# Regrouping q and k of the late chunks on the chip, by ScalarE copies of 32 partitions, in place of a regrouped copy in DRAM

## The chip, the cores and the metric

The kernel runs on 1 core of one Trainium2 chip. The metric is the device time of one execution in microseconds (us). An execution under the profiler gives a span, from the first to the last instruction, and a trace of every instruction and transfer.

## The reference

Two blocks follow each other. The first is a linear attention with a decay per head, over 4 batches, 8 heads, 768 positions and 64 columns a head:

```python
for b in range(nb):                       # blocks of 64 positions
    intra = einsum('bhic,bhjc->bhij', qb, kb) * Dmask
    intra = einsum('bhij,bhjd->bhid', intra, vb)
    inter = einsum('bhid,bhde->bhie', qb * lam_pow, kv_state)
    out[:, :, sl] = intra + inter
    kv_state = lam_block * kv_state + einsum('bhsd,bhse->bhde', kb * rev_pow, vb)
```

Its output, laid out as 3072 tokens of 512 columns, is the `x` of the second block, a sum over 4 experts weighted by normalised probabilities:

```python
for e in range(E):                        # w1[e]: 512 x 1024, w2[e]: 1024 x 512
    out += p[:, e:e + 1] * (maximum(x @ w1[e], 0.0) @ w2[e])
```

Everything is float32.

## The kernel before

The 3072 tokens are worked in three groups of 1024. A pair of a group and an expert is a unit, 12 in all. The products are done by a scheme of seven block products in place of eight, nested once more inside (names `M1` to `M7`, sums `S` and `T`), so that besides TensorE the other engines have many additions. While the products of one unit run, operands of the next ones are made and loaded.

The main loop (from L1850) goes over `at` (unit), `i` (one of seven products) and `x` (eight parts). One pass of the inner loop is called a slot here, and slot number `(at * 7 + i) * 8 + x` is what work around it is hung on. In the first units a slot of even `x` holds a part of `second_product` (L1233, eight matmul passes into a `q` bank), and a slot of odd `x` two inner products of `first_product` (L1174, into the banks `g1` and `g3`, tiles `pg`). What is read out of `g1` and `g3` is shared between VectorE (L117) and ScalarE: a copy at L1187, a seed of a bank from SBUF at L1151, the last part at L1155 or, with a ReLU, L1157; ReLUs in place are L1191 and L1094. Each engine runs its instructions in the order in which the program names them: an instruction that waits holds up all behind it on that engine.

The attention is cut into 24 chunks `n` of 128 positions of one batch (all 8 heads). Chunks 0 to 7 run ahead of the main loop, chunks 8 to 23 inside it, at the slots that `AT` (L888) lists. For a chunk, q and k must stand with the 64 columns of a head on partitions. Chunks up to 11 are turned by TensorE (L727) and copied out of PSUM by ScalarE (L735, L736). Chunks 12 to 23 ("come across", L506) use VectorE's transpose of 32 x 32 blocks (L707) instead. It transposes each block in place, so the blocks must first be moved: partition group `j` has to hold 32 columns of one half of the heads, and along the free dimension the four heads, and the four groups of 32 positions.

Before, this move is done in DRAM. `bring_across` (L490) lists 128 transfers from q and k to a DRAM tile `across`, in pieces of 32 floats; `trickle` (L501) issues them one by one, during the last direct products ahead of the loop and in the loop (L1963), from SyncE's queue or from ScalarE's. `load_across` (L509) then loads two regrouped tiles, `qx` and `kx`, a chunk. Besides, k is loaded as it stands (`kn`, L174), since the states need k with positions on partitions.

The steps of a late chunk with the slot `s` in `AT` are laid out in `attention` (L892). `turns_at` is `s - 7`, at which VectorE's transposes are queued (they go onto the list `lately` and are taken out at later slots) and at which `decayed` (L682) multiplies `kn` in place on GpSimd. Loads of q and k are at `turns_at - 5`, that of v at about `s - 7`, and at `s` stand the chunk's scores (L761, L768) and the values of the chunk before it (L824, L842, read out by L863). For chunks 12 to 23 `turns_at` is 51, 84, 92, 101, 108, 140, 147, 160, 165, 196, 203 and 216.

`small` (L92) takes tiles of 128 x 512 floats from one pool of 42 buffers. The tiles of q and k come from it, and so do the hidden blocks `m` of the products. A tile whose buffer is still in use waits for its last user.

`send` (L109) issues a transfer and adds an estimate of its time to counters by which `pump` (L208) decides when the next piece of background work ("chores": preparing weights on GpSimd, with their loads) is begun.

Of the kernel before, what the change touches and what calls it, by code (L numbers as in the profile page):

```python
# [14 lines left out]
FP32 = mybir.dt.float32  # L15
# [6 lines left out]
def kernel(  # L22
# [30 lines left out]
    nc = tc.nc  # L53

    B, H, S, D = q.shape
    E, DM, F = moe_w1.shape
    NTOK, DOUT = out.shape
    P = nc.NUM_PARTITIONS
    C = P
    BL = C // 2  # L60
    NHP = H // 2
    NCH = S // C
    CPG = 8
    G = CPG * C
    NG = NTOK // G
# [14 lines left out]
    dram = ctx.enter_context(tc.tile_pool(name="sums", bufs=1, space=DRAM))  # L80
# [11 lines left out]
    def small(name):  # L92
        return pool.tile([P, W], FP32, name=name, tag="t")
# [15 lines left out]
    def send(out, in_, by=None):  # L109
        n = 4 * min(packet(out), packet(in_))  # L110
        moved[0] = max(moved[0], now[0]) + 4 * math.prod(out.shape) / n * (9 + n / 25) / 16 / 1714
        if by is None:
            asked[0] = max(asked[0], now[0]) + 0.27
        (by or nc.sync).dma_start(out=out, in_=in_)
# [35 lines left out]
    def where(n):  # L150
        g, x = divmod(n, CPG)
        return (x // 4, x % 4) if g == 0 else (2 * g + x // 2 % 2, 2 * (x // 4) + x % 2)
# [5 lines left out]
    nat = {}  # L158
# [324 lines left out]


    FIRST_ACROSS = CPG + 4
    across = dram.tile([2, P, NHP, B, 16, 32], FP32, name="across")
    pieces = []
    rank = {0: 0, 2: 1, 3: 2, 1: 3}

    def bring_across(b):  # L490
        c = min(where(n)[0] for n in range(FIRST_ACROSS, NG * CPG) if where(n)[1] == b)
        for x, of in enumerate((q, k)):
            for y in range(4):
                for ac in range(NHP):
                    src = of[b, 4 * (y // 2) + ac, c * C:, (y % 2) * 32:(y % 2 + 1) * 32]
                    to = across[x, y * 32:(y + 1) * 32, ac, b, (c - 2) * 4:]
                    pieces.append((rank[b], lambda by, to=to, src=src: send(
                        out=to, in_=src.rearrange("(t p) d -> p t d", p=32), by=by,
                    )))

    def trickle(m=1, by=None):  # L501
        for _ in range(m):
            if pieces:
                pieces.pop(0)[1](by)

    def comes_across(n):  # L506
        return n >= FIRST_ACROSS

    def load_across(n):  # L509
        c, b = where(n)  # L510
        for x, name in enumerate("qk"):
            t = small(f"{name}x")
            send(
                out=t[:].rearrange("p (h c) -> p h c", c=C),
                in_=across[x, :, :, b, (c - 2) * 4:(c - 1) * 4].rearrange("p h t d -> p h (t d)"),
            )
            nat[n, name + "x"] = t

    def load_more(n):
        if not comes_across(n):  # L520
            load(n, "qk")
        else:
            trickle(sum(x <= rank[where(n)[1]] for x, _ in pieces))
            load_across(n)
            load(n, "k")

    first = small("zeros")
    zeros = first[:, 0:P]
# [36 lines left out]
    for r in range(2):  # L565
        for ac in range(NHP):
            h = 4 * r + ac
            nc.vector.tensor_tensor_scan(
                out=s_decay[:, r, ac], data0=lam_bc[:, h:h + 1].to_broadcast([P, BL]), data1=blk_ident,
# [10 lines left out]
    for ac in range(NHP):  # L580
        nc.vector.tensor_tensor_scan(
            out=q_decay[:, ac], data0=lam_q[:, ac:ac + 1].to_broadcast([P, BL]), data1=zeros[:, 0:BL],
# [303 lines left out]

    FILL = {1: 18, 2: 43}
    AT = (34, 40, 47, 53, 58, 91, 99, 108, 115, 147, 154, 167, 172, 203, 210, 223)  # L888
    V_AHEAD = {CPG + 10: 8, CPG + 13: 10}
    steps = []  # L890

    def attention():  # L892

        first, last = CPG, NG * CPG - 1
        for n in range(first, last + 1):
            s = AT[n - first]
            turns_at = s - (7 if comes_across(n) else 4)

            def both(n=n):
                if n > first:  # L900
                    values(n - 1, ("s0", "s1"))
                scores(n, ("q02", "q12"))

            steps.append((turns_at - (5 if comes_across(n) else 7), lambda n=n: load_more(n)))
            steps.append((s - V_AHEAD.get(n, 7), lambda n=n: load(n, "v")))
            steps.append((turns_at, lambda n=n: turn(n, ("s0", "s1"))))
            if comes_across(n):
                steps.append((turns_at, lambda n=n: (decayed(n), nat.pop((n, "k")))))
            steps.append((s, both))
        steps.append((AT[last - first] + 5, lambda: values(last, ("s0", "s1"))))  # L910
        steps.append((AT[last - first] - 14, turn_gates))
        steps.sort(key=lambda s: s[0])
# [888 lines left out]
        lambda: own_weights("M1"), sum_own("S1", "A21", "A22", ALU.add), *w2_steps[0:4], mine["M1"], *w2_steps[4:],  # L1801
        raw["A12"],
    ))
    for b in rank:
        bring_across(b)
    for m in SEQ0[2:]:
        if m == SEQ0[-1]:
            for _ in range(2):
                feed2(*fill2.pop(0))
        work = direct_product(m, blocks, ("g1", "g3")) if m != "M5" else [m5[1], *m5[3:]]  # L1810
        for x, f in enumerate(work):
            f()
            for y in sums_then.get((m, x), ()):
                y()
            rest()
            if x < len(work) - 1:
                now[0] += 1
                take(own_sums)
                pump(0.75)
            trickle()  # L1820

    start, w1_steps = now[0], prepare_w1(2)

# [26 lines left out]
    for at, (g, e) in enumerate(units):  # L1850
# [14 lines left out]
        for i in range(7):  # L1865
# [18 lines left out]
            else:  # L1884
                b = second_product(g, e, SEQ2[i], banks)
# [21 lines left out]
            for x, part in enumerate(order):  # L1907
                for f in part:
                    if f:
                        f()  # L1910
                now[0] += 1
                put = False
                if at == 0:
                    idle[:] = [("s0", "s1"), i < 3]
                    put = put_back()
                    take(own_sums)
                if nested and ahead:
                    idle[1] = x in ((1, 4) if i < 5 or at > NEST + 1 else (4,)) and (at - 2 * E + 1, i, x) not in held_at
                    put = put_back()
                added = first_steps.pop((at - 2 * E + 1, i, x), None)  # L1920
                if added:
                    added()
                all_added(now[0])
                if joins and not background:
                    joined()
                elif added and x > 2 or put:
                    pass
                elif (ahead or x % 2 == 0 and x + i) and not (nests and i == 6 and x == 7):
                    if nested or nests:
                        if lately:  # L1930
                            take(lately)
                        else:
                            rest()
                        if at == 2 * E and i in (2, 3) and fits():
                            rest()
                    else:
                        took = False
                        for of in (lately, background, own_sums):
                            if of and (not took or fits() or of is background and len(of) > 4):
                                take(of)  # L1940
                                if of is lately and i == 0:
                                    take(of)
                                took = True
                if nested or nests:
                    take(aside)
                    if own_sums and (nested or fits()):
                        take(own_sums)
                if ending and fits():
                    end_first()
                if nested and ahead and x in (1, 3) and fill3:  # L1950
                    feed3(*fill3.pop(0))
                if turned_back and x > 0:
                    for y in turned_back.pop(0):
                        if SEQ3[i] == END[1]:
                            give(*y[:2], ("s0", "s1"), *y[2:])
                        else:
                            give_across(*y)
                if fill and at * 7 + i >= 6 and x in ((0, 1) if at * 7 + i < 13 else (1, 3, 5) if at * 7 + i == 13 else FEED[nested]):
                    feed(*fill.pop(0))
                while steps and (at * 7 + i) * 8 + x == steps[0][0]:  # L1960
                    steps.pop(0)[1]()
                if at == 0 or x % 2 or at == 1 and x == 4:
                    trickle(1, nc.scalar if x % 2 else None)  # L1963
                for h in range(1, NG):
                    if x == 3 and 0 <= at * 7 + i - FILL[h] < 7:
                        x_fill(h, SEQ[at * 7 + i - FILL[h]])
                pump(PACE[g])
# [30 lines left out]
```

## Time and profile before

| what | value |
|---|---|
| median of 3 runs | 1142.18 us (1140.82 to 1142.65) |
| the profiled execution's own time | 1142.07 us |
| its span | 1140.3 us |
| mean granted TensorE clock | 0.999 |
| busy: TensorE, its weight loads, VectorE, ScalarE, GpSimd | 1130.5, 988.2, 769.0, 380.3, 761.0 us |
| transfers of `across`: issued by SyncE, by ScalarE | 61, 67 |
| size of one: 64 of 64 KB, 64 of 32 KB | 6.3 MB in all |
| loads of `qx` and `kx` | 24 of 256 KB, median 4.8 us to landing |
| loads of `kn` as it stands, late chunks | 12 of 256 KB, median 5.1 us to landing |
| VectorE's transposes of `qx` and `kx` | 24, median 700 ns each |

Busy time of an engine is the time in which at least one of its instructions runs; overlapping instructions count once. A wait in the profile is the time an engine stood idle before an instruction, put down to whatever released it last. A transfer's time to landing runs from its issue to its last byte. The share "DMA" is that of the 16 transfer engines' time in which they work at packets.

### The profile page before, as it was taken

The page shows a single profiled execution, that of the slowest core. Times are in us where ns is not written, and L with a number is a line of the kernel's source. Part 1 is how long each engine was busy: PE and PEld are TensorE (multiplying, and loading weights), DVE is VectorE, ACT ScalarE, POOL GpSimd, SP SyncE. Part 2 cuts the span into 40 slices and gives each one's busy share as a digit, 9 for nine tenths or more (in the row PEclk, how much of TensorE's full clock was granted, in tenths as well). Part 3 has the DMA queues.
Part 4 walks back from the last instruction along what each step waited for, and adds up shares of the span by engine and source line. Part 5 has one row for each costly group of instructions (what it writes and reads, how often), then busy time and mean ns, then how long its engine had stood idle before and what let it go on. Part 6 is the DMA issues. An engine that isn't in the chain of part 4 may idle for free.

```text
span 1140.3 us, 22080 instructions
## 1 busy us (share of the span) xinstructions
PE 1130.5 (99%) x7983; PEld 988.2 (87%) x7983; DVE 769.0 (67%) x1474; ACT 380.3 (33%) x768; POOL 761.0 (67%) x730
## 2 busy tenths in 40 slices
PE   8999999999999999999999999999999999999998
PEld 7888888888888888888888888888888888888887
DVE  4576776587577658737655566878767576776785
ACT  3325123212312321232343442444354452342332
POOL 2838147644843786447687997994996873873885
PEclk9999999999999999999999999999999999999999
DMA  9795889999899989769557858886577757657552
GB/s 204 180 287 166 212 222 279 291 270 335 262 292 320 316 291 282 222 222 314 177 177 261 283 180 281 290 272 204 180 264 244 218 162 207 194 160 211 171 194 74
DMA packets 326828, 267.12 MB, mean 234 GB/s; under 512 B 153216, under 2 KB 270144, under 8 KB 326720
## 3 DMA queue, kind: packets, MB, share of 16 engines
q1 hardware_dynamic: 289472, 258.14, 73.1%
q10 hardware_dynamic: 37216, 7.57, 3.5%
q8 instruction: 64, 1.05, 0.4%
q14 instruction: 44, 0.36, 0.1%
q0 software_dynamic: 32, 0.00, 0.0%
HBM read 197.97 MB, written 73.96 MB: 238 GB/s over the span
## 4 chain that ended last, share of the span: by engine, by line
PE 98%; DVE 1%; issue 0%; DMA 0%; ACT 0%; DVEq 0%; POOLq 0%; ACTq 0%
PE pg L1174 41%; PE pq L1550 25%; PE q L1233 21%; PE pM L1692 2%; PE pc L1692 2%; PE op L824 1%; PE sp L761 1%; PE op L842 1%; PE sp L768 1%; PE pM L1417 1%; PE pg L1550 1%; PE qp L727 1%; PE kp L727 0%; DMA decay<-in_lam_dram 0%; PE yp L1377 0%
## 5 line engine op out<-in xcount | busy, mean ns | idle before, releaser
L1174 PE MATMUL pg<-xs,ws_in 128*128 128x256 f32 x1960 | 470.1, 380 | 0.0
L1174 PEld LDWEIGHTS pg<-xs,ws_in 128*128 128x128 f32 x1960 | 371.1, 190 | 52.8 <-DVE m L117 2.4
L117 DVE TENSOR_TENSOR m<-pg,m 128x512 f32<-128x512 f32 x374 | 255.4, 685 | 92.4 <-PE pg L1174 82.5
L1233 PE MATMUL q<-w2t,m 128*128 128x256 f32 x1120 | 265.6, 380 | 0.0
L1233 PEld LDWEIGHTS q<-w2t,m 128*128 128x128 f32 x1120 | 211.7, 190 | 29.3 <-issue 0.3
L117 DVE TENSOR_TENSOR sums<-pq,sums 128x256 f32<-128x256 f32 x272 | 112.9, 420 | 90.6 <-PE pq L1550 76.9
L1550 PE MATMUL pq<-acc,w2t 128*128 128x256 f32 x688 | 169.2, 379 | 0.0
L117 POOL TENSOR_TENSOR m<-m,decay 128x512 f32<-128x512 f32 x91 | 114.5, 1270 | 78.7 <-ACT m L1191 52.1
L1550 PEld LDWEIGHTS pq<-acc,w2t 128*128 128x128 f32 x688 | 130.6, 190 | 17.9
L1191 ACT ACTIVATE m<-m 128x512 f32<-128x512 f32 x99 | 62.4, 630 | 192.5 <-DVE m L117 190.6
L1251 DVE SCALAR_TENSOR_TENSOR acc<-q,gate,acc 128x256 f32<-128x256 f32 x108 | 52.0, 482 | 79.1 <-PE q L1233 78.6
L117 DVE TENSOR_TENSOR m<-m,m 128x512 f32<-128x512 f32 x108 | 92.9, 861 | 6.5 <-ACT m L1157 6.5
L1187 ACT COPY m<-pg 128x512 f32<-128x512 f32 x88 | 51.5, 585 | 122.0 <-PE pg L1174 108.7
L1151 ACT COPY pg<-m 128x512 f32<-128x512 f32 x77 | 45.4, 590 | 113.0 <-DVE m L117 103.3
L117 POOL TENSOR_TENSOR acc<-hT,hT 128x512 f32<-128x512 f32 x56 | 70.3, 1272 | 15.0 <-PE pq L1550 9.9
L117 POOL TENSOR_TENSOR acc<-hT,acc 128x512 f32<-128x512 f32 x56 | 71.2, 1272 | 6.4 <-PE pq L1550 2.7
L1550 PE MATMUL pq<-hT,w2t 128*128 128x256 f32 x288 | 70.0, 379 | 0.0
L117 POOL TENSOR_TENSOR w2o<-w2b 128x512 f32<-128x512 f32 x26 | 33.9, 1325 | 45.8 <-DMA w2b<-in_moe_w_dram 39.3
L1550 PEld LDWEIGHTS pq<-hT,w2t 128*128 128x128 f32 x288 | 54.7, 190 | 7.4
L1155 ACT COPY m<-pg 128x512 f32<-128x512 f32 x44 | 25.7, 585 | 89.6 <-PE pg L1174 84.8
L1550 PE MATMUL pq<-m,w2t 128*128 128x256 f32 x228 | 55.4, 379 | 0.0
L1005 ACT COPY hp<-m 128x512 f32<-128x512 f32 x84 | 48.5, 589 | 15.6 <-DVE hT L117 14.1
(157 smaller groups left out, 1419.5 us busy)
## 6 DMA issues: line engine op xcount, KB each, us to landing
ws_in<-w_ops SPq DMA_DIRECT2D x40, 512.0 KB, 5.1
w2t<-w_ops SPq DMA_DIRECT2D x72, 256.0 KB, 3.2
ws_in<-w_ops SPq DMA_DIRECT2D x60, 256.0 KB, 3.5
ws_in<-w_ops SPq DMA_DIRECT2D x40, 384.0 KB, 4.0
w2b<-in_moe_w_dram SPq DMA_DIRECT2D x56, 256.0 KB, 5.0
w_ops<-ops SPq DMA_DIRECT2D x28, 512.0 KB, 5.5
w_ops<-ops SPq DMA_DIRECT2D x54, 256.0 KB, 4.3
w2t<-w_ops SPq DMA_DIRECT2D x100, 128.0 KB, 2.8
```

What stands on the lines that cost most here:

```text
L117: eng.tensor_tensor(out=o, in0=a, in1=b, op=op)
L727: nc.tensor.transpose(out=x[:, ac * C:(ac + 1) * C], in_=y[:, ac].rearrange("p r d -> p (r d)"), identity=ident[:],)
L1005: nc.scalar.copy(out=there[x][:], in_=blk[at][:])
L1151: nc.scalar.copy(out=banks[tags[1]][:], in_=new["11"][:])
L1155: nc.scalar.copy(out=o[:], in_=p[:])
L1174: nc.tensor.matmul(out=p[:, j * 256:(j + 1) * 256], lhsT=ws[i][:, j * P:(j + 1) * P], rhs=xs[i], start=(fresh and j == 0), stop=True, skip ...
L1187: nc.scalar.copy(out=new[at][:], in_=p[:])
L1191: nc.scalar.activation(out=new[at][:], in_=new[at][:], func=AF.Relu)
L1233: nc.tensor.matmul(out=p[:, s * DH:(s + 1) * DH], lhsT=h[A_OF[m]][:, c * 256 + s * P:c * 256 + (s + 1) * P], rhs=fed2[g, e, m][uu][:, c], ...
L1251: nc.vector.scalar_tensor_tensor(out=o, in0=x, scalar=w, in1=o, op0=ALU.mult, op1=ALU.add)
L1550: nc.tensor.matmul(out=p[:, 0:256], lhsT=fed3[e, m, i][:, c * P:(c + 1) * P], rhs=b[B_OF[i]][:, c * 256:(c + 1) * 256], start=(fresh and c ...
L1692: nc.tensor.matmul(out=p[:, s * 256:(s + 1) * 256], lhsT=a[c][:, f:f + P], rhs=b[:, c, j * 256:(j + 1) * 256], start=(s == 0 and c == 0 an ...
```

## The change

The tile `across` goes, with `bring_across`, `trickle`, `load_across` and every call of them. For a late chunk q is loaded as it stands, like k, into one more tile from the pool, 13 slots ahead of `turns_at`, and k 9 slots ahead. In the eight slots ahead of `turns_at` a new function `regroup` issues four ScalarE copies a slot, first four slots for q, then four for k. A copy takes 32 partitions and 4 heads x 32 columns (128 elements a partition) to another group of 32 partitions of a new tile, `qx` or `kx`, the same tiles that VectorE's transposes then take. The tile of q is let go after its last copy; that of k stays for the states.

```diff
-    across = dram.tile([2, P, NHP, B, 16, 32], FP32, name="across")
...
     def load_more(n):
         if not comes_across(n):
             load(n, "qk")
-        else:
-            trickle(sum(x <= rank[where(n)[1]] for x, _ in pieces))
-            load_across(n)
-            load(n, "k")
+
+    def regroup(n, name, part):
+
+        of = nat[n, name]
+        if part == 0:
+            nat[n, name + "x"] = small(name + "x")
+        to = nat[n, name + "x"][:].rearrange("p (h t c) -> p h t c", h=NHP, c=32)
+        for j in (2 * part, 2 * part + 1) if SPLIT == 2 else (part,):
+            r, d = j // 2, j % 2 * 32
+            for t in range(4):
+                nc.scalar.copy(
+                    out=to[j * 32:(j + 1) * 32, :, t], in_=of[t * 32:(t + 1) * 32, :, r, d:d + 32],
+                )
+        if part == SPLIT - 1 and name == "q":
+            del nat[n, name]
...
+    SPLIT = 4
+    AHEAD = 13, 9
...
-            steps.append((turns_at - (5 if comes_across(n) else 7), lambda n=n: load_more(n)))
+            if comes_across(n):
+                steps.append((turns_at - AHEAD[0], lambda n=n: load(n, "q")))
+                steps.append((turns_at - AHEAD[1], lambda n=n: load(n, "k")))
+                for x in range(2 * SPLIT):
+                    steps.append((turns_at - 2 * SPLIT + x, lambda n=n, x=x: regroup(n, "qk"[x // SPLIT], x % SPLIT)))
+            else:
+                steps.append((turns_at - 7, lambda n=n: load_more(n)))
...
-    for b in rank:
-        bring_across(b)
...
-            trickle()
...
-                if at == 0 or x % 2 or at == 1 and x == 4:
-                    trickle(1, nc.scalar if x % 2 else None)
```

More of the change, by code (lines that the diff above doesn't have):

```diff
@@ L485 @@
     FIRST_ACROSS = CPG + 4
-    across = dram.tile([2, P, NHP, B, 16, 32], FP32, name="across")
[L487 to L504, printed above, removed]
     def comes_across(n):
         return n >= FIRST_ACROSS
[L509 to L517, printed above, removed]
     def load_more(n):
```

## The prediction

> **What bounds the kernel now.** I read the page's busy times, then the chain of waits, then the busy time by stage over the stretch that the change touches (46 us, where the first transfer to `across` is issued, to 500 us, where the last late chunk ends).
>
> ```profile
> PE 1130.5 (99%) x7983; PEld 988.2 (87%) x7983; DVE 769.0 (67%) x1474; ACT 380.3 (33%) x768; POOL 761.0 (67%) x730
> ...
> PE 98%; DVE 1%; issue 0%; DMA 0%; ACT 0%; DVEq 0%; POOLq 0%; ACTq 0%
> ```
>
> ```profile
> 170.00:250.00 80.00, 79.85 (x728) 69.78 (x727) 52.39 (x100) 19.53 (x42) 51.70 (x58) 1.00 0.94 280
> 250.00:330.00 80.00, 78.84 (x836) 68.98 (x835) 54.47 (x109) 19.94 (x45) 45.21 (x53) 1.00 0.94 298
> 330.00:410.00 80.00, 80.00 (x811) 69.84 (x810) 57.41 (x108) 20.22 (x46) 50.72 (x57) 1.00 0.96 298
> 410.00:500.00 90.00, 90.00 (x794) 78.45 (x796) 63.77 (x111) 19.77 (x43) 50.72 (x54) 1.00 0.82 257
> ```
>
> The columns are stage, length, then busy us of PE, PEld, DVE, ACT and POOL, the granted clock, the DMA share and GB/s. TensorE is busy 328.7 of 330 us. The transfer engines are nearly full too (0.82 to 0.96), but nothing on TensorE waits for them. A busy TensorE could still be stretched, so I looked at its order of time: eight passes of L1233 or L1174 start every 1.73 us throughout (in the last fence 373.44, 375.16, 376.89), 216 ns a pass against 190 ns of weight load. That is its pace also after 500 us, where the change does nothing. What is left to win is therefore TensorE's waits. From 46 to 500 us these are all:
>
> ```profile
> PE sp L761 <- issue: 1.2, 1, 1.2
> PE pc L1692 <- DVE xs L117: 0.7, 1, 0.7
> PE op L824 <- DVE qT L117: 0.2, 1, 0.2
> ```
>
> In sum 2.1 us, 0.18% of the time. Whatever the change takes off DMA or SyncE, it can hardly win more.
>
> **What it removes.** 128 transfers and the loads from `across`:
>
> ```profile
> L114 ACTq DMA_DIRECT2D across<-in_k_dram x37: 557/558/668, 90.8 to 328.9; - x37
> L114 SPq DMA_DIRECT2D across<-in_q_dram x34: 551/610/1609, 46.2 to 273.0; - x34
> L114 ACTq DMA_DIRECT2D across<-in_q_dram x30: 557/558/1382, 103.8 to 276.9; - x30
> L114 SPq DMA_DIRECT2D across<-in_k_dram x27: 552/567/1308, 68.7 to 288.8; - x27
> ```
>
> The three numbers are the shortest, median and longest ns of an issue. ScalarE loses 67 x 0.56 = 37 us of issuing. SyncE loses 61 x 0.6 = 37 us, and 24 loads of `qx` and `kx` less 12 new loads of q, 12 x 0.6 = 7 us, and its waits for `across` to land (19.9 and 10.7 us in the list of SyncE's waits, since the loads must follow the copies). On the transfer engines 6.3 MB in pieces of 128 bytes are 49,152 packets. The page gives the ScalarE queue 37,216 packets for 3.5% of 16 engines' span, that is 0.035 x 1140.3 x 16 / 37,216 = 17 ns a packet; so about 49,152 x 17 ns / 16 = 52 us of the whole set, of some 247 us (0.87 x 284) at work between 46 and 330 us. None of it is on TensorE's path, so it is worth between 0 and 2.1 us. The wait of 1.2 us at L761 (267.2 to 268.6 us) has no releaser in the profile and falls where the DMA share is over 1.0; it may be late because of that load or not. I take half of it: **-0.6 us**.
>
> **What it adds on ScalarE.** 12 chunks x 32 = 384 copies, SBUF to SBUF, 32 partitions, 128 elements. The trace has none of this form; the nearest are these, and a row of four in order of time:
>
> ```profile
> L863 ACT COPY xc<-op 128x128 f32<-128x128 f32 x64 | 12.2, 277 | 31.4 <-PE op L842 31.3
> L625 ACT COPY decay<-decay 128x16 f32<-128x16 f32 x4 | 0.6, 200 | 0.0
> ```
>
> ```profile
> 367.04 0.75 ACT L863 COPY xc<-op 128x128 f32<-128x128 f32 x4
> ```
>
> One copy of 128 elements lasts 277 ns, but four in a row last 0.75 us: the next starts 0.16 us after the last ((0.75 - 0.277) / 3). From SBUF, `decay` of 16 elements starts every 0.106 us (its rows in order of time, 69.80, 69.91, 70.01, 70.12) and 512 elements (`hp<-m` and `jp<-sums`, in a row) every 0.52 us; a straight line between gives 0.106 + 112 x (0.414 / 496) = 0.20 us for 128. Bounds: 0.16 (all that the row of four shows) and 0.277 (no overlap). I take **0.20 us**, as it is from SBUF like the copies: 77 us in all, 0.8 a slot, 6.4 a chunk. A product of eight slots lasts some 13 us (four times 1.73 for L1233, 28 passes x 216 ns for L1174), so 1.62 us a slot: 0.8 a slot fits beside what ScalarE does now, a quarter of the time.
>
> [...]
>
> Where do 0.8 us a slot hurt? Not where the copies are alone, but in slots 157 to 159, where the last three slots of chunk 19 and the first three of chunk 20 coincide (100, 139 and 195 coincide singly): eight copies a slot. I walked ScalarE's queue there, with these rows:
>
> ```profile
> 370.10 0.63 ACT L1191 ACTIVATE m<-m 128x512 f32<-128x512 f32 x1 [2.32 <-DVE m L117]
> 370.64 0.58 ACT L1151 COPY pg<-m 128x512 f32<-128x512 f32 x1
> 372.63 0.63 ACT L1191 ACTIVATE m<-m 128x512 f32<-128x512 f32 x1 [1.41 <-DVE m L117]
> 374.75 0.63 ACT L1094 ACTIVATE m<-m 128x512 f32<-128x512 f32 x1 [1.49 <-DVE m L117]
> 375.42 0.63 ACT L1191 ACTIVATE m<-m 128x512 f32<-128x512 f32 x1
> 375.95 0.58 ACT L1157 ACTIVATE m<-pg 128x512 f32<-128x512 f32 x1
> ```
>
> ```profile
> 373.44 1.89 PE L1174 MATMUL pg<-xs,ws_in 128*128 128x256 f32 x8
> 375.16 1.89 PE L1233 MATMUL q<-w2t,m 128*128 128x256 f32 x8
> 376.89 1.89 PE L1174 MATMUL pg<-xs,ws_in 128*128 128x256 f32 x8
> ```
>
> In the program's order, 8 copies (slots 155 and 156) come behind the L1191 of 370.10, 8 (157) behind that of 372.63, 8 (158) behind the L1094 of 374.75. A large one lets the next begin after 0.54 us. At 0.20: copies 370.64 to 372.24; the seed L1151 to 372.76; L1191 to 373.30; copies to 374.90; L1094 to 375.44; copies to 377.04; L1191 to 377.58; L1157 from 377.58 to 378.16. TensorE wants that bank with the second half of the group of 376.89, at 377.75: 0.4 us and the semaphore, **+0.45 us**. At 0.16, L1157 ends at 377.7: nothing. At 0.277 (with large ones at their full 0.63) it ends at 380.45: +2.7. Elsewhere a slot's lag of 0.8 to 1.6 us is hidden by the same 1.2 us from the end of L1157 (376.53) to 377.75, by two slots between a seed and its product, and for the `xc` copies by the slot after them; taken at 0, if that cover went at each of the three other coinciding slots, some 0.5 us each, +1.5.
>
> VectorE's transposes now wait for ScalarE instead of a load. They follow `turns_at` by 2 to 12 us (51 to 380.94 us: `kx` of chunk 19, whose copies end by the same walk at 380.3); nothing. GpSimd's `decayed` writes k in place and now waits for k's last copy; its product of 1.06 us is wanted only 7 slots (11 us) later.
>
> **What it moves: the loads.** q goes to SyncE's queue 5 slots ahead of its first copy, k too: 5 to 6 slots of 1.62 us, 8 to 9.7 us, for a landing of 5.1 us (row of `kn`). So SyncE may run up to 3 to 4.6 us behind. Before, `kn` was issued 1.8 to 11.3 us behind the slot that names it (worst chunk 15: named when TensorE was at 258.9, issued at 270.19), with one ahead. Per chunk, (37 + 7 + 30.6) / 12 = 6 us of SyncE's time go, so the lag should fall under 5 us mostly. A late load blocks ScalarE's whole queue, read-outs of `g1` and `g3` included; 1.2 us of that are covered. I assume two or three of 24 loads late by 1 to 2 us: **+0.3 us**, bounds 0 and 11.3 - 4.6 - 1.2 = +5.5.
>
> **Sum.** -0.6 + 0.45 + 0.3 = +0.15 on 1142.07, its own time with 1.8 us around the span and 0.1 under the median: 1142.2; with the median's 0.1, **1142.3 us**.
>
> **The rivals.**
>
> *SyncE is held by the pool (slower).* Counting first and last uses in the program's order, 42 of the 42 buffers are taken around slots 88 to 91, 146 to 148 and 198; the change holds one to three more per chunk in the eight slots ahead of `turns_at - 5`. The loads of q for chunks 15 (slot 88) and 19 (slot 147) must then wait for a release that comes later in the program, two to three slots (3 to 5 us), and all loads of SyncE stand behind. It costs from the point where a `w2t`, `ws_in` or q is late by more than its cover: 5 us twice less 1.2 each, and something at chunk 22, some +5 to +8: 1148. For it: the full pool; against: SyncE lagged 6 to 11 us there before without a wait on TensorE. 0.18.
>
> *Copies do not overlap (slower).* Then +2.7 and the three other slots +1.5, less 0.6: 1145.7. [...] Against it, the row of four in 0.75 us. 0.10.
>
> *The background work falls otherwise (slower).* With `send` no longer counting `across`, `pump` begins chores earlier; GpSimd and SyncE get another order, and a `kd` or a `ws_in` comes late a few times, each 0.5 to 1.3 us as now on other waits: +3, 1145. For it: VectorE is busy 12.2 of 14 us from 337 to 351 us, with little room; against: the chores' list is paced by GpSimd, not by transfers. 0.10.
>
> *DMA relief shows (faster).* All 2.1 us go, and VectorE's and weight loads' small waits: -2.6, 1139.5. Against it: the wait on `xs` is VectorE's own. 0.07.
>
> **The numbers.** My forecast, no change that can be told, 0.55, with its own range 1140.8 to 1144.4. A measurement of this kernel tells about 0.2% (2.3 us) from no change. Faster 0.07; same 0.55; slower 0.18 + 0.10 + 0.10 = 0.38. The range of 8 in 10 goes from 1140.6 to 1148.5: under it the last rival, over it the tail of the first.
>
> **What would show it.** Right: TensorE's waits from 46 to 500 us stay under some 3 us, none of over 1 us on a `pg` or `q` bank; the new copies start some 0.2 us apart in a row; the DMA share from 170 to 330 us falls to about 0.8. The walk: L1157 near 376 us is late by 1.6 us. Wrong: TensorE waiting for ScalarE's L1157, L1155 or L1187, or for `ws_in` and `w2t`; ScalarE standing before a copy for `qn` or `kn`; SyncE waiting for a TensorE product before `qn`.

## The result, and the profile after

| | before | after |
|---|---|---|
| median, same chip | 1141.86 us (1140.82 to 1142.65, 4 runs) | 1156.29 us (1156.18 to 1157.13, 4 runs) |
| profiled execution, span | 1142.07, 1140.3 us | 1156.36, 1154.5 us |
| mean granted TensorE clock | 0.999 | 0.996 |

The change makes the kernel slower: ratio 1.0129, 95% interval 1.0111 to 1.0146, +14.4 us. The forecast was 1142.3 us, no change that can be told, with a range up to 1148.5 us; the kernel after lies 7.8 us above the top of it.

Lines of the program after stand 10 to 20 lower: the new copies are L502, the `pg` products L1163 (before L1174), the `q` products L1222 (L1233), the seed L1140 (L1151), the last part with ReLU L1146 (L1157), the ReLUs in place L1180 and L1083 (L1191, L1094), the read-out of values L844 (L863).

First the page of after: the busy times, the shares in the chain of waits, and the two groups of new copies (busy us, mean ns of one, then the idle time before them).

```profile
PE 1136.0 (98%) x7983; PEld 989.1 (86%) x7983; DVE 767.9 (67%) x1474; ACT 493.4 (43%) x1152; POOL 763.0 (66%) x730
...
PE 87%; ACT 4%; DVE 2%; DMA 2%; POOL 2%; issue 1%; SPq 1%; DVEq 0%; POOLq 0%; ACTq 0%
...
L502 ACT COPY kx<-kn 32x128 f32<-32x128 f32 x192 | 56.7, 295 | 3.7 <-DMA kn<-in_k_dram 1.4
L502 ACT COPY qx<-qn 32x128 f32<-32x128 f32 x192 | 56.7, 295 | 3.2 <-PE q L1222 0.5
```

ScalarE's busy time rose by 493.4 - 380.3 = 113.1 us, the whole 56.7 + 56.7 = 113.4 us of the copies: 384 x 295 ns. A busy time counts overlapping instructions once, so copies that cover each other would have shown less. The chain of waits was 98% TensorE and now has 4% of ScalarE in it: an engine that is busy 43% of the span sets the time in places.

Next the busy time by stage of after (the columns are those of the table in the prediction).

```profile
170.00:250.00 80.00, 79.13 (x721) 68.36 (x720) 50.59 (x99) 42.79 (x121) 54.91 (x60) 1.00 0.83 267
250.00:330.00 80.00, 78.15 (x831) 67.51 (x830) 54.04 (x107) 43.52 (x126) 49.00 (x54) 1.00 0.88 281
330.00:410.00 80.00, 75.62 (x678) 64.64 (x680) 53.93 (x99) 53.56 (x162) 51.10 (x57) 0.96 0.84 261
410.00:500.00 90.00, 87.27 (x729) 75.32 (x720) 60.02 (x112) 47.75 (x139) 50.90 (x59) 1.00 0.80 245
```

TensorE stands idle 0.87 + 1.85 + 4.38 + 2.73 = 9.8 us here, against 330 - 328.7 = 1.3 us before. The transfer engines did get relief, as their share fell from 0.94 to 0.83 and 0.88, but TensorE gained nothing from it here. From 330 to 410 us the granted clock is 0.96, where the same four stages of before had 1.00. Whom TensorE waited for (us in total, times, longest), from 46 to 520 us, less two waits of 0.4 us each:

```profile
PE pg L1163 <- ACT m L1146: 6.0, 6, 3.2
PE pg L1163 <- ACT pg L1140: 3.0, 3, 1.4
PE pc L1681 <- DVE xs L117: 0.6, 1, 0.6
```

The waits for ScalarE are nine, 9.0 us in all, every one for a bank that it had to read out or to seed. They end at 247.8, 276.5, 280.7, 347.3, 351.6, 385.4, 455.3, 459.7 and 491.7 us, each within a burst of copies. The longest, of 3.22 us, is the place that the prediction walked through, where chunks 19 and 20 coincide. There ScalarE in order of time (start us, length of the row, instructions):

```profile
376.23 1.22 ACT L502 COPY kx<-kn 32x128 f32<-32x128 f32 x4
377.47 0.59 ACT L1140 COPY pg<-m 128x512 f32<-128x512 f32 x1
377.99 0.62 ACT L1180 ACTIVATE m<-m 128x512 f32<-128x512 f32 x1
378.63 1.22 ACT L502 COPY kx<-kn 32x128 f32<-32x128 f32 x4
379.86 1.22 ACT L502 COPY qx<-qn 32x128 f32<-32x128 f32 x4
381.10 0.63 ACT L1083 ACTIVATE m<-m 128x512 f32<-128x512 f32 x1
381.74 1.22 ACT L502 COPY kx<-kn 32x128 f32<-32x128 f32 x4
382.96 1.22 ACT L502 COPY qx<-qn 32x128 f32<-32x128 f32 x4
384.21 0.63 ACT L1180 ACTIVATE m<-m 128x512 f32<-128x512 f32 x1
384.75 0.58 ACT L1146 ACTIVATE m<-pg 128x512 f32<-128x512 f32 x1
```

and TensorE in order of time (in brackets the idle time before and who ended it):

```profile
381.13 1.03 PE L1163 MATMUL pg<-xs,ws_in 128*128 128x256 f32 x4
385.38 2.08 PE L1163 MATMUL pg<-xs,ws_in 128*128 128x256 f32 x4 [3.22 <-ACT m L1146]
387.25 3.62 PE L1222 MATMUL q<-w2t,m 128*128 128x256 f32 x8
390.66 2.13 PE L1163 MATMUL pg<-xs,ws_in 128*128 128x256 f32 x8
392.63 0.59 PE L1222 MATMUL q<-w2t,m 128*128 128x256 f32 x2
```

ScalarE has no gap at all: it is not waiting, it is full. Four copies last 1.22 us, so the last begins (1.22 - 0.295) / 3 = 0.31 us after the third: no overlap. L1146 stands behind all of them in program order and ends at 384.75 + 0.58 = 385.33; TensorE starts at 385.38. Behind the wait TensorE goes on at half speed: eight passes take 390.66 - 387.25 = 3.41 us where they take 1.73 elsewhere, and the granted clock from 386 to 391 us is 0.50.

### The profile page after: what moved, and what is told of

It is laid out like the page before. It is cut to its first block, busy times and chain, and to the rows that moved or that the text cites. A ratio compares the mean times of both kernels' runs of the same rounds, so it can differ in the third digit from the quotient of the medians.

```text
span 1154.5 us, 22358 instructions
## 1 busy us (share of the span) xinstructions
PE 1136.0 (98%) x7983; PEld 989.1 (86%) x7983; DVE 767.9 (67%) x1474; ACT 493.4 (43%) x1152; POOL 763.0 (66%) x730
## 4 chain that ended last, share of the span: by engine, by line
PE 87%; ACT 4%; DVE 2%; DMA 2%; POOL 2%; issue 1%; SPq 1%; DVEq 0%; POOLq 0%; ACTq 0%
PE pg L1163 37%; PE pq L1539 24%; PE q L1222 17%; PE pc L1681 2%; ACT qx L502 2%; DVE m L117 1%; PE pM L1681 1%; ACT kx L502 1%; SPq L114 1%; POOL ops L117 1%; PE op L805 1%; PE sp L742 1%; ACT m L1180 1%; PE op L823 1%; PE sp L749 1%
## 5 line engine op out<-in xcount | busy, mean ns | idle before, releaser
L1163 PE MATMUL pg<-xs,ws_in 128*128 128x256 f32 x1960 | 473.9, 381 | 9.5 <-ACT m L1146 6.0
L1163 PEld LDWEIGHTS pg<-xs,ws_in 128*128 128x128 f32 x1960 | 371.0, 190 | 66.2 <-ACT m L1146 7.4
L1222 PE MATMUL q<-w2t,m 128*128 128x256 f32 x1120 | 267.3, 382 | 0.0
L1222 PEld LDWEIGHTS q<-w2t,m 128*128 128x128 f32 x1120 | 212.9, 191 | 29.8 <-issue 0.3
L1180 ACT ACTIVATE m<-m 128x512 f32<-128x512 f32 x99 | 62.4, 630 | 137.4 <-DVE m L117 131.7
L117 DVE TENSOR_TENSOR m<-m,m 128x512 f32<-128x512 f32 x108 | 88.3, 818 | 20.1 <-ACT m L1146 14.5
L1140 ACT COPY pg<-m 128x512 f32<-128x512 f32 x77 | 45.3, 588 | 106.6 <-DVE m L117 99.1
L117 POOL TENSOR_TENSOR kn<-kn,decay 128x512 f32<-128x512 f32 x16 | 17.4, 1087 | 78.6 <-ACT kx L502 30.2
L502 ACT COPY kx<-kn 32x128 f32<-32x128 f32 x192 | 56.7, 295 | 3.7 <-DMA kn<-in_k_dram 1.4
L502 ACT COPY qx<-qn 32x128 f32<-32x128 f32 x192 | 56.7, 295 | 3.2 <-PE q L1222 0.5
```

Of the source, the lines that this page charges most:

```text
L117: eng.tensor_tensor(out=o, in0=a, in1=b, op=op)
L502: nc.scalar.copy(out=to[j * 32:(j + 1) * 32, :, t], in_=of[t * 32:(t + 1) * 32, :, r, d:d + 32],)
L1140: nc.scalar.copy(out=banks[tags[1]][:], in_=new["11"][:])
L1163: nc.tensor.matmul(out=p[:, j * 256:(j + 1) * 256], lhsT=ws[i][:, j * P:(j + 1) * P], rhs=xs[i], start=(fresh and j == 0), stop=True, skip ...
L1180: nc.scalar.activation(out=new[at][:], in_=new[at][:], func=AF.Relu)
L1222: nc.tensor.matmul(out=p[:, s * DH:(s + 1) * DH], lhsT=h[A_OF[m]][:, c * 256 + s * P:c * 256 + (s + 1) * P], rhs=fed2[g, e, m][uu][:, c], ...
```

## The experiments

Two questions come out of this. Why does a copy take 0.31 us from start to start, when the prediction had taken 0.20? And do the late banks make the whole loss, or does some of it come from the loads, the pool of 42 buffers or the order of the background work? The edits are to the kernel after, unless said otherwise. The first four kernels shared their runs of before (median 1143.51 us).

**Same copies, no move between partition groups.** This reads from the group that it writes to; the blocks therefore stay in their groups, and the scores of the late chunks are those of other data. The number and shape of the copies, waits and loads are as in after.

```diff
-                    out=..., in_=of[t * 32:(t + 1) * 32, :, r, d:d + 32],
+                    out=..., in_=of[j * 32:(j + 1) * 32, :, r, d:d + 32],
```

> Every copy of the changed kernel reads the partition group that it writes (j in place of t): as many copies, of the same shape, size and place in the queue, but four in a row stay on one group of 32 partitions; the regrouping itself is left out, so q and k are wrong. Theory A (a copy cannot begin before the last has ended because its partition group differs from the last one's): copies start about 0.20 us apart within a part, ScalarE's busy time falls from 493 to about 455 us, TensorE's waits for L1146 and L1140 (9 us) nearly go, time 1142 to 1145. Rival B (a copy of 128 elements from SBUF never overlaps): still 0.307 us apart, time 1155 to 1157. Rival C (loads and buffers, not the copies, make the loss): whatever the spacing, time above 1152.

Measured: 1143.76 us (1141.91 to 1146.15, 10 runs), ratio to before 1.0004, interval 0.9991 to 1.0018. The page, and then ScalarE in order of time at the same place:

```profile
PE 1131.8 (99%) x7983; PEld 988.7 (86%) x7983; DVE 775.1 (68%) x1474; ACT 464.8 (41%) x1152; POOL 762.9 (67%) x730
...
L502 ACT COPY qx<-qn 32x128 f32<-32x128 f32 x192 | 42.8, 292 | 3.1 <-DMA qn<-in_q_dram 2.1 <-PE q L1222 0.3
```

```profile
377.20 0.89 ACT L502 COPY kx<-kn 32x128 f32<-32x128 f32 x4
378.10 0.89 ACT L502 COPY qx<-qn 32x128 f32<-32x128 f32 x4
379.02 0.63 ACT L1180 ACTIVATE m<-m 128x512 f32<-128x512 f32 x1
379.55 0.58 ACT L1146 ACTIVATE m<-pg 128x512 f32<-128x512 f32 x1
```

Each copy is nearly as long as in after (292 ns) but the next begins (0.89 - 0.292) / 3 = 0.20 us later: the spacing that the prediction had worked out. The same 384 copies are then 85.6 us of busy time instead of 113.4, and the loss is gone. TensorE still waits once for L1146, for 1.5 us. So the loss hangs on the 0.11 us between 0.31 and 0.20, not on the loads, the pool or the order, which are the same in both kernels.

**One large copy in place of sixteen.** The regroup is left out: at its first part one copy of 128 x 512 with the halves of the heads and their rows exchanged stands in its place, so again the scores are of other data. Loads, tiles and the planner are as in after.

```diff
+        if part == 0:
+            to = nat[n, name + "x"][:].rearrange("p (r i d) -> p r i d", r=2, d=D)
+            nc.scalar.copy(out=to, in_=of.rearrange("p i r d -> p r i d"))
-        for j in (2 * part, 2 * part + 1) if SPLIT == 2 else (part,):
...
```

> The 16 copies of a tile are replaced by one of 128 partitions x 512 elements at the first of their four slots; the regrouping is left out, loads, buffers, their slots and all waits stay. Theories A and B (ScalarE's time in copies): 24 copies of 0.59 us, 14 us in place of 118, TensorE's waits for ScalarE go, time 1140.5 to 1142.5. Rival C (SyncE held by the full pool, loads late): the same waits of SyncE as in the changed kernel, time stays above 1150. Rival D (background work begun at other times): above 1145 with waits on GpSimd.

Measured: 1141.19 us (1140.10 to 1143.29, 10 runs), ratio 0.9982, interval 0.9969 to 0.9996. TensorE's waits from 46 to 520 us:

```profile
PE pc L1677 <- DVE xs L117: 0.4, 1, 0.4
PE pg L1159 <- DVE m L117: 0.4, 1, 0.4
PE op L801 <- DVE qT L117: 0.2, 1, 0.2
```

With one copy in place of sixteen everything else that the change does is a small gain. SyncE still waits for products of TensorE before its loads of q and k (L174). The longest such wait, in after and then in this kernel, is that of chunk 15's q:

```profile
SPq L174 <- PE op L805: 8.4, 1, 8.4
SPq L174 <- PE op L801: 6.7, 1, 6.7
```

Before, no load at this line stood over 0.5 us. SyncE's waits for products of L1222 (in this kernel L1218) rose too, from 22.8 us in before to 83.2 in after, and are 72.8 here; by the names of the tiles, 70 of the 83.2 and 66 of the 72.8 are transfers into `w2t`, which has six buffers of its own, so they are not waits for the pool of 42. None of all that reaches TensorE. The time, 0.18% under before, is about what a faster regroup could reach within this plan of loads.

**Chunk 19 three slots earlier.** This parts chunk 19 from chunk 20 and leaves the number of copies alone.

```diff
+                early = 3 if n == 19 else 0
-                steps.append((turns_at - AHEAD[0], lambda n=n: load(n, "q")))
+                steps.append((turns_at - early - AHEAD[0], lambda n=n: load(n, "q")))
...
```

> Loads and copies of chunk 19 alone stand three slots earlier, so that no slot holds copies of both 19 and 20. Theories A and B: the wait of 3.2 us on L1146 near 382 us goes and with it the stretch of half clock behind it (13 passes at 0.43 us, 2.7 us); the other waits stay: 1149 to 1151.5. Rival C: the load of q of chunk 19 asks for a buffer while the pool is full, so no better or worse: 1155 or more.

Measured: 1153.28 us (1153.06 to 1153.68, 4 runs), ratio 1.0084, interval 1.0062 to 1.0106; span 1151.3 us, mean clock 1.000. TensorE's waits from 46 to 520 us, less one of 0.4 us:

```profile
PE pg L1164 <- ACT m L1147: 3.5, 6, 1.1
PE pg L1164 <- ACT pg L1141: 2.7, 3, 1.4
PE pg L1164 <- DVE m L117: 1.7, 3, 0.9
```

The wait of 3.2 us is down to 1.1 at most, and the clock stays whole, yet that is only 3.2 us of span (1154.5 to 1151.3), less than expected: waits on VectorE rose from 0.4 to 1.7 us. Part of the 3.2 us is the clock: an execution of after whose clock stayed whole, shown below, has a span of 1152.5 us, only 1.2 us over this one. The place where three slots of two chunks coincide is the worst one and the smaller part of the loss; 0.84% of the 1.29% is left without it.

**The copies of k by GpSimd.** ScalarE keeps the 192 copies of q.

```diff
-                nc.scalar.copy(
+                (nc.scalar.copy if name == "q" else nc.gpsimd.tensor_copy)(
```

> k's 192 copies run on GpSimd, q's on ScalarE. Theories A and B: ScalarE has 16 copies a chunk (4.9 us of 13), its read-outs are late by less than 1.2 us: TensorE's waits for it under 2 us, 1143 to 1146, if a copy on GpSimd takes 0.3 us or less; where it takes 0.6 us or more (192 x 0.6 = 115 us on an engine that is 66% busy) GpSimd's own work comes late, 1148 to 1160, with waits on POOL in place of ACT. Rival C: above 1152 with SyncE's waits as before.

Measured: 1153.87 us (1151.46 to 1154.97, 3 runs), ratio 1.0079, interval 1.0045 to 1.0113. The group of the page, then TensorE's one large wait, then VectorE's:

```profile
L502 POOL COPY kx<-kn 32x128 f32<-32x128 f32 x192 | 66.4, 346 | 11.0 <-DVE m L117 2.8
```

```profile
PE pg L1163 <- DVE m L117: 6.7, 5, 2.7
```

```profile
DVE kx L688 <- POOL kx L502: 20.4, 7, 6.0
```

TensorE no longer waits for ScalarE, which has the lighter load, but 6.7 us for VectorE. VectorE in turn stands 20.4 us before its transposes for GpSimd's copies, and its read-outs of banks stand behind them in its order. So half the copies, moved to GpSimd, seem to have made a new wait two engines further on that gave back most of what the old one had cost. That chain is read from the waits; no run takes it apart.

**Which change of group costs?** In after a slot's four copies write one group `j` and read groups 0 to 3. The first experiment took two things away together: the move from one group into another, and the change of the read group from copy to copy. The next kernel lets the four copies of a slot read one group and write all four in turn; all copies are still made.

```diff
-            for t in range(4):
-                nc.scalar.copy(out=to[j * 32:..., :, t], in_=of[t * 32:..., :, r, d:d + 32])
+        t = part
+        for j in range(4):
+            r, d = j // 2, j % 2 * 32
+            nc.scalar.copy(out=to[j * 32:..., :, t], in_=of[t * 32:..., :, r, d:d + 32])
```

> The same 16 copies of a tile, in the other order: the four of a slot share the group they read (t) and change the group they write (j); the result is right. In the changed kernel they share the group they write and change the one they read. If only a change of the group that is read holds a copy back, copies start 0.20 us apart in a slot, ScalarE's busy time falls to about 465 us and the time to 1142 to 1146, as where both groups stay. If a change of either group holds it back, 0.307 us and 1155 to 1157.

Measured: 1156.3 us (1153.7 to 1158.56, 4 runs), ratio 1.0111, interval 1.0073 to 1.0148 (median of before in the same set of runs 1143.31). A slot's four copies:

```profile
170.18 1.21 ACT L502 COPY qx<-qn 32x128 f32<-32x128 f32 x4
```

1.21 us, 0.307 from start to start throughout: a change of the written group alone holds the next copy just as a change of the read group does.

**Both groups change with each copy.**

```diff
+            for t in range(4):
+                j = (t + part) % 4
```

> The same copies in a diagonal order, in which each of the four of a slot changes both the group that it reads and the one that it writes; the result is right. If the price is that of waiting for the end of the copy before, it is paid once: 0.307 us and 1154 to 1158, as in the changed kernel. If each change has a price of its own, 0.40 us and 1165 or more.

One run: 1155.56 us, span 1153.6, the time expected for 0.307 us a copy and not the 1165 of 0.40; 56.7 us a group again, that is 192 x 295 ns with no overlap. The price is paid once, whichever changes.

**Across groups, but the same two groups in a row.** The move across partitions is kept (written group `j`, read group `j + 1`) and only the change from copy to copy is taken away; the blocks so come from other rows than they should.

```diff
-                    out=..., in_=of[t * 32:(t + 1) * 32, :, r, d:d + 32],
+                    out=..., in_=of[(j + 1) % 4 * 32:((j + 1) % 4 + 1) * 32, :, r, d:d + 32],
```

> As the kernel that stays in one group, but each copy reads the group next to the one that it writes, and the four of a slot keep both; the regrouping is left out again. If only a change of group from one copy to the next holds a copy back, 0.20 us from copy to copy in a slot, and 1142 to 1146. If a copy from one group to another is what cannot overlap, 0.307 us and 1154 to 1158.

One run: 1144.26 us, span 1142.4 (a single run of before beside it took 1149.69, so the time by itself tells little; the trace decides here). The group of the page, and a slot's four copies:

```profile
L502 ACT COPY kx<-kn 32x128 f32<-32x128 f32 x192 | 42.8, 292 | 4.9 <-DMA kn<-in_k_dram 4.2
```

```profile
169.60 0.89 ACT L502 COPY qx<-qn 32x128 f32<-32x128 f32 x4
```

42.8 us again, 0.20 from start to start, and 1.3 us of waiting for L1146. To copy from one group into another costs nothing by itself; to change the groups from one copy to the next does. Counted over copies that follow each other with nothing between: in after some 323 of 339 begin 0.30 or 0.31 us apart; here 284 begin 0.20 apart and 39, at the border of two slots where `j` changes, 0.30 (a row of eight with one such border, from 174.38 us, lasts 1.80 us).

**The copies for q alone.** From the kernel before: k keeps its copy in DRAM, q is regrouped on the chip, so that 192 of the copies are left.

```diff
-        for x, of in enumerate((q, k)):
+        for x, of in ((1, k),):
...
-        for x, name in enumerate("qk"):
+        for x, name in ((1, "k"),):
...
+                steps.append((turns_at - 13, lambda n=n: load(n, "q")))
+                for x in range(4):
+                    steps.append((turns_at - 8 + x, lambda n=n, x=x: regroup(n, x)))
```

> q is regrouped by ScalarE as in the changed kernel, k through the DRAM tile as before; the result is right. Half the copies (192, 59 us of ScalarE), in four slots of a chunk, so that no two chunks coincide. Theory A: 4 x 0.307 = 1.23 us a slot of 1.62 us, but only for four slots (6.5 us) at a time, so the lag of ScalarE's queue stays near the 1.2 us of cover: 1142 to 1146, TensorE's waits for ScalarE under 3 us. If the loss went with the number of copies: half of 14 us, 1149.

Measured: 1147.15 us (1144.81 to 1149.86, 10 runs), ratio 1.0026, interval 1.0005 to 1.0048. TensorE's waits from 46 to 520 us:

```profile
PE pg L1192 <- POOL ops L117: 2.4, 1, 2.4
PE pg L1192 <- DVE m L117: 1.1, 2, 0.8
PE pg L1192 <- ACT m L1175: 1.0, 3, 0.5
PE pg L1192 <- ACT pg L1169: 0.5, 1, 0.5
```

Half of the copies leave 1.0 + 0.5 = 1.5 us of waits on ScalarE, not half of 9.0, although each copy still pays the full 0.307 us (56.6 us in its group). That is what one expects of a full queue: behind four slots of copies four free ones let it drain, and no two chunks coincide. The time is somewhat over what was expected. A part of it stands ahead of the first copy, which starts at 170.1 us (TensorE in order of time):

```profile
104.54 1.85 PE L1192 MATMUL pg<-xs,ops 128*128 128x256 f32 x4 [2.38 <-POOL ops L117]
106.19 2.90 PE L1251 MATMUL q<-w2t,m 128*128 128x256 f32 x8
```

The wait of 2.4 us for GpSimd's `ops` can't be of the copies' making; the order of the background work may be its cause. Behind it the passes are slower: the four take 106.19 - 104.54 = 1.65 us, where the four behind a wait in after take 0.97 (276.50 to 277.47 us), and the row of eight lasts 2.90 us in place of 1.89. So the wait and the slow passes cost some 4 us here (2.38 + 0.68 + 1.01). Whether they are there in each execution is open.

**After once more.**

> The changed kernel itself beside the three others, unchanged, for comparison on the same chip: 1155 to 1158, 0.307 us from copy to copy.

Measured: 1155.88 us (1154.4 to 1158.31, 4 runs), ratio 1.0115, interval 1.0072 to 1.0158; profiled span 1152.5 us, mean clock 1.000. TensorE in order of time at the long wait:

```profile
385.14 1.13 PE L1163 MATMUL pg<-xs,ws_in 128*128 128x256 f32 x4 [3.20 <-ACT m L1146]
386.11 1.89 PE L1222 MATMUL q<-w2t,m 128*128 128x256 f32 x8
387.84 1.89 PE L1163 MATMUL pg<-xs,ws_in 128*128 128x256 f32 x8
389.57 0.81 PE L1222 MATMUL q<-w2t,m 128*128 128x256 f32 x3
```

The same wait, to 0.02 us, and then full pace. From the end of the wait 20 passes take 389.57 - 385.14 = 4.43 us here. In the first profile of after the same 20 run from 385.38 to 392.63, where the next L1222 starts: 7.25 us. The difference of 2.8 us is the half clock, and it is more than the difference of the two spans (2.0 us). So the half clock is no part of the loss in each execution.

## Why the prediction was wrong

**The step that failed** is the price of one copy: "I take **0.20 us**, as it is from SBUF like the copies", with 0.277 as its upper bound. Measured: 0.307 from start to start, above the bound. The rows that it came from (`decay`, `hp`, `jp`, and the row of four `xc`) all read and write all 128 partitions, one after the other. They show how instructions overlap that begin at the same partitions. Of an instruction that begins in another group than the last, the trace of before has no row for ScalarE, and the text took the two for the same. For the case that it really priced, 0.20 us was right: the kernels with the same groups and with the steady move measured it. The bound "no overlap" was set at the length of another instruction (277 ns); the new copies are 295 ns long.

**The walk was right with that price put in.** From 370.64 us with 8 copies in 2.46 us, and the rest as it stood, L1157 would end at 380.74, and TensorE wants the bank at 377.75: +3.0 us. Measured: 3.22. The 0.2 us more are two ReLUs behind which a copy began after 0.64 us in place of 0.54 (377.99 to 378.63 and 381.10 to 381.74). The text had +0.45, from 1.6 us for 8 copies.

**"Elsewhere" was the larger mistake in the sum**: "taken at 0", +1.5 at the worst. A slot lasts 1.62 us and ScalarE's other work takes a quarter of it, 0.4 us. With 0.8 us of copies that leaves room; with 4 x 0.307 = 1.23 us it is 1.63 us of work in 1.62. Each slot of a chunk's eight is then full, and the lag that one coinciding slot makes isn't worked off in the slots behind it. So the cover went: behind slots 100, 139 and 195, where two chunks coincide singly, TensorE waited for a seed and, some 4 us later, for L1146, 1.41 + 0.44, 0.64 + 0.52 and 0.95 + 0.62 us, 4.6 us in all where the text had at most three times 0.5 and had called the seeds covered. Two more waits, 0.44 us at 247.8 and 0.73 at 491.7, came where nothing coincides, the first where the copies of chunk 14 follow those of chunk 13 at once.

**The sum again.** Of the 14.2 us by which the span grew, TensorE's idle time from 170 to 500 us is 9.8 - 1.3 = 8.5, and its busy time grew by 1136.0 - 1130.5 = 5.5. Of the latter 2.8 is the half clock behind the long wait. Another 1.5 or so is a matter of counting: a pass that nothing follows is recorded as 0.38 us where the next would start after 0.216, some 0.16 at each of nine waits. Some 0.9 us more are the first four passes behind such a wait, which take 0.1 us longer than elsewhere (0.97 us from 276.50 to 277.47, for 0.86). About 0.3 us are not accounted for.

**The rivals.** "Copies do not overlap" (0.10, 1145.7 us) was the right mechanism, but too cheap at 0.277 us and with a lag at three places only. The 384 copies of 295 ns are the 113 us by which ScalarE's busy time grew. Yet the same copies with their groups left alone overlap, at 0.20 us, so neither their 128 elements nor reading from SBUF keeps them apart. "SyncE is held by the pool" (0.18) came true as a wait: the q of chunk 15, which the text named, stood 8.4 us for a product of TensorE, and SyncE's other transfers behind it. It had no cost that shows: with one large copy 6.7 us of it remain and the ratio is 0.9982. "The background work falls otherwise" (0.10) may have cost the 2.4 us on `ops` in the profile with q alone, and nothing that after shows on TensorE. "DMA relief shows" (0.07) is small at most: with one large copy 0.18%, some 2 us (interval 0.04 to 0.31%), about the bound of 2.1 us that the text had read off TensorE's waits; that it comes from the transfers is not shown.

**The rest held.** The loads of q and k cost ScalarE 1.4 + 0.3 us of standing, for a term of +0.3 us on the path; the DMA share fell to 0.83 and 0.88 for "about 0.8"; the wait of 1.2 us at L761 is gone. What the text named as proof against itself (waits of over 1 us on a `pg` bank, TensorE waiting for L1157, copies not 0.2 us apart) is what came.

**No better version was found.** The kernels with the same groups, with one large copy and with the steady move leave the regroup out, wholly or in part, and only the one large copy is under before, by 0.18%. An order of the copies in which q and k alternate, so that two at a time keep their groups, needs two more tiles at once from the full pool and wasn't tried.

## What to carry to other kernels

A price per instruction taken from rows in a sequence holds for a sequence of that kind only: rows that all begin at partition 0 (they gave 0.20 us here) do not price copies that hop between groups of 32 (0.307 us). For an engine that runs in order, compare its work per slot with the slot over the whole burst; at 1.63 us in 1.62 no cover of 1.2 us lasted here (9.0 us of waits for ScalarE), at half the burst it nearly did (1.5 us). If one unknown price (0.20 or 0.31 us) decides between hidden and not hidden, that price belongs in the range with its full weight.

## What the runs showed of the hardware

**In these runs ScalarE held a copy that begins in another partition group than the instruction before it.** A copy of 32 x 128 floats, SBUF to SBUF, started 0.20 us after the last when both its groups were those of the last copy (same groups), and 0.307 us after it (its length of 0.295 and 0.012 more) when the read group (after) or the written group (loops swapped) differed. Where both differed, time (1155.56 us) and busy time (56.7 us a group) were as in after. With a steady move between two groups copies started 0.20 us apart, as within one. The hold was there behind a ReLU of 128 partitions too. In after the 21 copies that follow such a ReLU at once and write group 1, 2 or 3 started 0.63 to 0.65 us after it (377.99 to 378.63 us); the three that read and write group 0 (behind the ReLUs of 281.87, 366.38 and 474.53 us) started 0.54 us after it, like another instruction of 128 partitions (384.21 to 384.75).

**TensorE lost half its clock behind a wait of 3.22 us in one execution of after, and not behind one of 3.20 us in another.** In the first, eight passes took 3.41 us instead of 1.73, and the window from 386 to 391 us had a granted clock of 0.50; in the other the clock of that window was 1.00. Shorter waits went both ways. Behind 2.38 us with q alone a row of eight passes lasted 2.90 us instead of 1.89; with the copies of k on GpSimd, where the longest wait was 2.7 us, the clock was 0.98 from 330 to 410 us and 1.00 in the other three stages. Behind the wait of 1.41 us in after it was 1.00 (276 to 280 us). What decides here stays open.
